# The first pair of FFN tiles closed before the second is opened, and the parameters turned between its two halves

## The chip, the cores and the metric

The kernel runs on one core of a Trainium2 chip. The metric is the device time of one execution in microseconds (us), taken as the median of several runs; lower is better.

## What is computed

The input x has 2048 tokens of 448 features (bf16). Two branches read the same x and are mixed token by token with a gate g; the result is bf16, 2048 x 448.

```python
g = sigmoid((x * gate_w).sum(-1, keepdims=True))
# branch a: a diagonal complex state-space model (S5), 448 states
dt = exp(log_dt);  Lam_bar = exp(dt * (Lambda_re + 1j * Lambda_im))
B_bar = ((Lam_bar - 1.0) / Lam)[:, None] * (B_re + 1j * B_im)
Bu = einsum("bld,pd->blp", x, B_bar)
h[t] = Lam_bar * h[t - 1] + Bu[:, t]          # for t in range(2048)
a = 2.0 * einsum("blp,dp->bld", h, C_re + 1j * C_im).real + x * Dskip
# branch b: a feed-forward network, 448 -> 1792 -> 448
b = einsum("bsf,fd->bsd", silu(einsum("bsd,df->bsf", x, w1)), w2)
return g * a + (1 - g) * b
```

## The kernel before

The tokens are cut into four chunks (tc = 0 to 3) of 512. x is held turned (`xT`, features on partitions), 448 features in four blocks of 128 rows of which the last two overlap, so that every contraction is made of half blocks of 64 rows.

**The x products** (`x_products`, matmuls on L733) give two kinds of output tiles of 128 x 512: `F` tiles (x times w1, then SiLU on ACT, L703, into `aT`) and `B` tiles (x times B, copied to `UG` by DVE or ACT, L710/L712). Tiles are taken in pairs. The two tiles of a pair lie in two banks of PSUM and run side by side, one on the upper 64 rows of TensorE's array and one on the lower 64. A pair needs 14 half blocks, done as 7 steps of two matmuls: a first half of 4 steps, `half(k, 0)`, and a second half of 3 steps, `half(k, 1)`. In the second half the two tiles have changed their places between upper and lower rows, so a matmul of the second half writes a bank which the other half of the array has just written. The second half therefore waits for the first half's last matmul (`.own = h == 1`: the one case in which `Waits.put` makes PE wait on its own semaphore). In the loop the first half of the next pair is put between the two halves of a pair. `wait` names the exception: for k - 1 in `wait`, pair k is closed before pair k + 1 is opened. `fill` names other work which is put behind half n of a given k.

The first call does F tiles 0 to 9 of chunk 0, the seven B tiles of chunk 0, F tiles 10 to 13, and the B tiles of chunk 1. Pair 0's first half alone is issued as two pieces of two steps, each with the waits for what it reads; every other half is one piece and waits at its beginning for all that it reads. w1 comes in five column cuts (`W1CUTS`), each in two transfers (the upper and the lower two row blocks), all on SyncE's (SP's) queue but one: cut 0 holds pair 0, cut 1 pair 1, cut 2 pairs 2 and 3, cut 3 pair 4 and one tile more.

**The parameters** (`parameters`, fill `PRMF`): log_dt, Lambda_re and Lambda_im land as three rows of `prm`, are turned by four small matmuls against the identity (L605, `prm_t`) so that states lie on partitions, and are copied to `pc` (L609). The fourth block of columns wants columns 384 to 447 twice, on partitions 0 to 63 and 64 to 127; a DVE copy (L607) writes the second set into `prm` ahead of the turning. From `pc` hang the step sizes (GpSimd, i.e. POOL, L612), the phases (DVE, L624 and L593 to L631), and the sine and cosine tables (ACT, L629 and L632).

**The scan** (`lanes(tc)`): DVE multiplies `UG` by COS and SIN (L774), runs seven scans (L806), POOL's queue casts their results back into `UG` by DMA, and DVE turns them into `H` (L774).

**The gates** (`gates(tc)`, priority `GPR[tc]`): DVE products x * gate_w (`xg`) and x * Dskip (L774); ACT sums (L906), tanh (L908), g and 1 - g (L909, L910), and g * x * Dskip (L913).

**The rest**: `ffn2(tb)` multiplies `aT` by w2 for 128 tokens (L844), ACT evicts it times 1 - g (`fe`, L850), POOL's queue adds it to `xnat` (L852). `readout_weights` scales C (ACT `ct`, L891/L892, not before the planned time `CTAT`; DVE L894). `readout(tb)` multiplies `H` by it (L865); the result goes out (L875 and SP's stores).

**What sets the order.** The kernel lists its operations, and a planner (`Plan.order`) orders them ahead of time, with costs and priorities written in the code. PE keeps the order in which the operations are listed; on ACT, DVE, POOL and SP the operation that can start first by the plan goes next, and among those that can start at once the one with the lower priority number (silu 2.5, sines 3, fe 7, gates and ct 8 on ACT; phases 0 to 3, gates `GPR`, lanes 20 + tc on DVE). At run time each engine does its list in that order, waiting on semaphores. The planner also gives out the eight PSUM banks.

Of the kernel before, what the change touches and what calls it, by code (L numbers as in the profile page):

```python
# [11 lines left out]
BF16 = DT.bfloat16  # L12
# [14 lines left out]
XT1K = 6  # L27
S0 = (0, 4, 1, 5, 2, 6, 3)
XT1 = "da"
XDMA = (1, 2, 3)  # L30
XAFT = ["PO1"]
LORD = "Bs w3 BQ BI w4 x1 g n1 w2 x2 C n2 n3".split()
BPE = ((3,4),)
TRATE = 2
MERGE = True
NHF = 10
# [3 lines left out]
GAT = 10  # L40
GEARLY = (2,)
GMID = ()
W1CUTS = [0,256,512,1024,1408,1792]
L2AT = 1
UDVE = (0, 1, 2, 3, 4, 5, 6)
OUTA = (8, 9, 10, 11)
PRMF = (1, 0)
PRMP = 9.7
CPP = 20.5
CTAT = 46.0  # L50
GPR = (14, 20.3, 20.4, 21.4)
CASTB = (360000, 360000, 360000)
XCOL = [0, 128, 256, 320]

# [254 lines left out]
def bass_gated_mix__ssm_conv_s5__dense_activation_silu__prompt_kernel(nc, A_x, A_Lambda_re, A_Lambda_im, A_B_re, A_B_im, A_C_re, A_C_im,  # L309
               A_log_dt, A_Dskip, B_x, B_w1, B_w2, gate_w, out):  # L310
    with ExitStack() as ctx:
# [3 lines left out]
        def sb(name, shape, dtype):  # L315
            return E(nc.sbuf_tensor(name, list(shape), dtype))
# [27 lines left out]
        ident = sb("ident", [128, 128], BF16)  # L344
# [5 lines left out]
        sgn = sb("sgn", [128, 1], F32)  # L350
        sturn = sb("sturn", [128, 1], F32)
        hpi = sb("hpi", [128, 1], F32)
        prm = sb("prm", [3, 512], BF16)
        eul = sb("eul", [128, 4], F32)
        pc = sb("pc", [128, 4, 4], F32)
        dtc = sb("dtc", [128, 4], F32)
# [31 lines left out]
        def bk(t, k=0):  # L388
            return ps[:, t.bank + k, :]
# [16 lines left out]
        def DVE(fn, r, w, cost, prio, tag=""):  # L406
            return P.add("dve", fn, r, w, cost, prio, tag=tag)
# [4 lines left out]
        def PE(fn, r, w, cost, tag=""):  # L412
            return P.add("pe", fn, r, w, cost, 0, tag=tag)
# [7 lines left out]

        w1cuts = W1CUTS

# [33 lines left out]
        def turn_x(tc, after=()):  # L457
            for c, n in ((0, 3), (3, 1)):
                turn(xT[:, tc, c:c + n, :], x2[tc * CH:(tc + 1) * CH, XCOL[c]:XCOL[c] + 128 * n], " ".join(f"xT{tc}_{q}" for q in range(c, c + n)), CH * 256 * n, 3.9 if n == 3 else 1.4, after)
# [138 lines left out]
        def parameters():  # L598

            prmn = [f"prm{k}" for k in range(3)]  # L600
            tkp = Ps()

            def prm_t(pe):
                for b in range(4):
                    r = pe.matmul(bk(tkp)[:, 4 * b:4 * b + 3], prm[0:3, 128 * b:128 * b + 128], ident[0:3, 0:3], start=True, stop=True)  # L605
                return r
            DVE(lambda e: e.tensor_copy(prm[:, 448:512], prm[:, 384:448]), prmn + ["xT0_211"], ["prm4"], 0.17, 0)  # L607
            PE(prm_t, prmn + ["prm4", "ident"], [tkp], 0.5, "prmT")
            DVE(lambda e: e.tensor_copy(  # L609
                pc[:, 0:3, :], bk(tkp)[:, 0:16].rearrange("p (b k) -> p k b", k=4)[:, 0:3, :]), [tkp], ["pc"], 0.2, 0)  # L610
            LDT, LRE, LIM = (pc[:, k, :] for k in range(3))
# [76 lines left out]
        def weights(tile, p0, p1, i):  # L688
            kind, tc, k = tile
            return w1s[p0:p1, i, k * 128:k * 128 + 128] if kind == "F" else BT[p0:p1, i, LCOL[k]:LCOL[k] + 128]  # L690
# [26 lines left out]
        def x_products(tiles, fill={}, wait=()):  # L717

            part = (list(zip([(i, 64) for i in (0, 1, 2, 3)], [(i, 0) for i in (0, 1, 3, 2)])),
                    list(zip([(i, 0) for i in (0, 1, 2)], [(i, 64) for i in (0, 1, 3)])))
            pairs = [tiles[t:t + 2] for t in range(0, len(tiles), 2)]
            toks = [Ps(2) for _ in pairs]

            def steps(k, h, a, z):
                def body(pe):
                    for n, cut in list(enumerate(part[h]))[a:z]:  # L730
                        for b, ((i, p0), tile) in enumerate(zip(cut, pairs[k])):
                            tc = tile[1]
                            r = pe.matmul(bk(toks[k], b), weights(tile, p0, p0 + 64, i), xT[p0:p0 + 64, tc, i, :],  # L733
                                          start=(h == 0 and n == 0), stop=(h == 1 and n == 2))
                    return r
                reads = [n for cut in part[h][a:z] for (i, _), tile in zip(cut, pairs[k])
                         for n in xn_of[tile[1]][i] + (w1n(tile[2], i) if tile[0] == "F" else btn[tile[2]])]
                return PE(body, list(dict.fromkeys(reads)), [toks[k]], (z - a) * PE_MM[512], f"{pairs[k][0][0]}{pairs[k][0][1]}")

            def half(k, h):  # L740
                if h == 0 and pairs[k][0] == ("F", 0, 0):
                    def zero(pe):
                        for n in range(NFILL):
                            for b, p in enumerate((slice(64, 128), slice(0, 64))):
                                r = pe.matmul(bk(toks[k], b)[:, 0:128], ones[p, 0:128], ones[p, 0:128], start=True, stop=True)
                        return r
                    PE(zero, [], [toks[k]], NFILL * 0.11, "fill")
                    steps(k, 0, 0, 2)
                    steps(k, 0, 2, 4)
                else:  # L750
                    steps(k, h, 0, len(part[h])).own = h == 1
                if h:
                    evict(pairs[k], toks[k])

            half(0, 0)
            for f in fill.get(-1, ()):
                f()
            for k in range(len(pairs)):
                order = [lambda: half(k, 1)] + [lambda: half(k + 1, 0)] * (k + 1 < len(pairs))
                for n, f in enumerate(order if k - 1 in wait else order[::-1]):  # L760
                    f()
                    for m in fill.get((k, n), ()):
                        m()
                for f in fill.get(k, ()):
                    f()
# [115 lines left out]
        def readout_weights(k):  # L881
# [15 lines left out]
        def gates(tc):  # L897
            xnn = ["xn00", "xn01"] if tc == 0 else [f"xn{tc}"]
            b4 = slice(4 * tc, 4 * tc + 4)
            tt(xg[:, :, :], xnat[:, b4, :], gwb[:, None, :].to_broadcast([128, 4, D_MOD]), ALU.mult,  # L900
               xnn + ["gwb"] + (["Gf0"] if tc else []), ["xg"], 1792, GPR[tc], "xg")
            tt(xnat[:, b4, :], xnat[:, b4, :], dkb[:, None, :].to_broadcast([128, 4, D_MOD]), ALU.mult,
               xnn + ["dkb"] + (["Gf0"] if tc else []), [f"xd{tc}"] + xnn, 1792, GPR[tc], "xd")
            for b in range(4):
# [11 lines left out]
        def xt(tc, who):  # L916
            return [lambda: x_transposes(tc, who)]
# [7 lines left out]
        def C(*tbs):  # L925
            return [lambda tb=tb: readout(tb) for tb in tbs]

        turn_b = [lambda a=a, z=z: b_transposes(a, z, "da") for a, z in BPE]
        NH = NHF
        K = NH // 2  # L930
        x_products(F(0, 0, NH) + B(0) + F(0, NH) + B(1),
                   {PRMF: [parameters], (K - 2, 0): turn_b[:1], K - 2: turn_b[1:2], K - 1: turn_b[2:], XT1K: xt(1, XT1) if 1 not in XDMA else [], 8: [lambda: lanes(0)] + [lambda: turn_x(3, XAFT)] * (3 in XDMA and bool(XAFT))}, [K - 2])
        gates(0)
        gates(1)
        for tc in GEARLY:
# [63 lines left out]
```

## Time and profile before

| | |
|---|---|
| median of 3 runs | 138.13 us (138.05 to 138.46) |
| the profiled execution | 138.0 us |
| its span, first to last instruction | 136.2 us |
| granted TensorE clock | 1.00 |
| PE, DVE, ACT, POOL busy | 97%, 87%, 65%, 31% of the span |
| matmuls of x products, L733 | 588 |
| matmuls of FFN 2, L844 | 224 |
| matmuls of the readout, L865 | 126 |

Reading it: times are from the span's start. PE is TensorE's matmuls, PEld its weight loads (which run beside matmuls), DVE VectorE, ACT ScalarE, POOL GpSimd, SP SyncE; a q behind an engine's name means its instruction queue, which issues DMAs and waits. A row of the timeline has the start, the length, engine, line, operation, names, shape and count of a group, and in brackets the engine's idle time ahead of it with what ended that. The chain of work that ended last is followed back from the end of the run, each piece to what released it. In a table by stage each engine has its busy time and its number of instructions, then the granted clock, the DMA engines' share and GB/s.

### The profile page before, as it was taken

Reading aid. Unit: us, or ns where it says so; the run is one execution under the profiler, and the core shown is the slowest. Engines: PE = TensorE matmul, PEld = TensorE weight load, DVE = VectorE, ACT = ScalarE, POOL = GpSimd, SP = SyncE. Lnnn points to the kernel's source line nnn. Section 1 sums busy time; section 2 is a strip of 40 time slices with the busy share of each in tenths; the row PEclk is TensorE's granted clock in tenths of the full one; section 3 lists DMA queues with packets and bytes.
Section 4 is the critical chain, followed back from the end, with each engine's and each line's share of the span. In section 5 each row is a group of like instructions: output and inputs, shape, how many; then the busy total and the mean of one; then the engine's idle time right before and its main releaser. Section 6 shows DMA issues by size and latency. Waiting matters only on the chain.

```text
span 136.2 us, 2554 instructions
## 1 busy us (share of the span) xinstructions
PE 132.4 (97%) x993; PEld 63.9 (47%) x993; DVE 118.5 (87%) x159; ACT 88.1 (65%) x155; POOL 42.0 (31%) x76
## 2 busy tenths in 40 slices
PE   7999999999999999999999999999999999999991
PEld 2444444444444555554444444445555555555561
DVE  0318999999997699999999999999999999999252
ACT  3238956999988997998476677699501117983200
POOL 7224030300346222224775020633100422346310
PEclk9999999999999999999999999999999999999999
DMA  4997989999999694222898010375712233229842
GB/s 125 334 240 135 205 129 262 343 176 155 206 212 234 110 183 75 36 34 34 119 141 155 3 39 0 54 110 109 153 65 95 39 52 49 32 38 130 171 108 68
DMA packets 29602, 16.87 MB, mean 124 GB/s; under 512 B 15123, under 2 KB 29462, under 8 KB 29590
## 3 DMA queue, kind: packets, MB, share of 16 engines
q1 hardware_dynamic: 22400, 10.38, 34.4%
q0 software_dynamic: 6640, 5.97, 29.2%
q10 hardware_dynamic: 550, 0.36, 0.8%
q8 instruction: 8, 0.13, 0.4%
q14 instruction: 4, 0.03, 0.1%
HBM read 5.62 MB, written 1.84 MB: 55 GB/s over the span
## 4 chain that ended last, share of the span: by engine, by line
PE 93%; DMA 3%; SPq 1%; issue 0%; DVE 0%
PE ps L733 46%; PE ps L844 31%; PE ps L865 16%; DMA w1s<-in_B_w_dram 3%; SPq L420 1%; DVE ot L875 0%; PE ps L605 0%; PE ps L673 0%
## 5 line engine op out<-in xcount | busy, mean ns | idle before, releaser
L733 PE MATMUL ps<-xT,w1s 64*128 64x512 bf16 x392 | 47.5, 376 | 0.3 <-DMA w1s<-in_B_w_dram 0.3
L844 PE MATMUL ps<-w2s,aT 128*128 128x448 bf16 x224 | 42.9, 352 | 0.0
L703 ACT ACTIVATE aT<-ps 128x1024 bf16<-128x1024 f32 (+1 forms) x30 | 28.7, 965 | 13.1 <-PE ps L733 12.9
L844 PEld LDWEIGHTS ps<-w2s,aT 128*128 128x128 bf16 x224 | 21.8, 98 | 20.7 <-issue 0.4
L733 PEld LDWEIGHTS ps<-xT,w1s 64*128 64x128 bf16 x392 | 20.0, 94 | 23.5 <-DMA w1s<-in_B_w_dram 0.7
L733 PE MATMUL ps<-xT,BT 64*128 64x512 bf16 x196 | 25.8, 376 | 0.0
L806 DVE TENSOR_TENSOR_SCAN Gf<-rc,gin,H 128x512 f32<-128x512 f32 x21 | 25.5, 1267 | 0.1
L852 POOL DMA_DIRECT2D xnat<-fe x16 | 13.8, 861 | 35.6 <-ACT fe L850 34.1
L420 POOL DMA_DIRECT2D UG<-Gf x27 | 15.0, 571 | 27.3 <-DVE Gf L806 26.8
L865 PE MATMUL ps<-CP,H 128*128 128x448 bf16 (+2 forms) x126 | 21.7, 332 | 0.0
L850 ACT ACTIVATE fe<-ps,g 128x448 bf16<-128x448 f32 x16 | 10.0, 626 | 17.8 <-PE ps L844 17.2
L865 PEld LDWEIGHTS ps<-CP,H 128*128 128x128 bf16 x126 | 11.6, 98 | 10.0 <-DVE Gf L806 0.4
L774 DVE TENSOR_TENSOR H<-UG,COS 128x3584 bf16<-128x3584 bf16 (+2 forms) x9 | 16.2, 1810 | 0.0
L733 PEld LDWEIGHTS ps<-xT,BT 64*128 64x128 bf16 x196 | 10.8, 94 | 11.5
L712 ACT ACTIVATE UG<-ps 128x1024 bf16<-128x1024 f32 (+1 forms) x12 | 10.7, 920 | 2.4 <-PE ps L733 2.4
L875 DVE SCALAR_TENSOR_TENSOR ot<-ps,g,xnat 128x448 bf16<-128x448 f32 (+2 forms) x14 | 8.1, 608 | 4.1 <-issue 2.8
L774 DVE TENSOR_TENSOR PO<-UG,SIN 128x1536 bf16<-128x1536 bf16 (+1 forms) x8 | 8.5, 1084 | 1.9 <-DMA UG<-Gf 1.9
L906 ACT ACTIVATE junk<-xg 128x448 bf16<-128x448 bf16 x16 | 9.2, 575 | 1.1 <-DVE xg L774 0.9
L420 POOL DMA_DIRECT2D UG<-UG x8 | 4.6, 575 | 17.1 <-ACT UG L712 9.6
L913 ACT ACTIVATE xnat<-xnat,g 128x448 bf16<-128x448 bf16 x16 | 9.7, 659 | 0.1
L774 DVE TENSOR_TENSOR PI<-UG,SIN 128x1536 bf16<-128x1536 bf16 (+1 forms) x8 | 8.6, 1086 | 0.0
L774 DVE TENSOR_TENSOR H<-H,PI 128x3584 bf16<-128x3584 bf16 x4 | 8.1, 2022 | 0.1
(93 smaller groups left out, 95.0 us busy)
## 6 DMA issues: line engine op xcount, KB each, us to landing
UG<-Gf POOLq DMA_DIRECT2D x21, 128.0 KB, 2.9
xnat<-fe POOLq DMA_DIRECT2D x16, 112.0 KB, 2.6
w2s<-in_B_w_dram SPq DMA_DIRECT2D x1, 1568.0 KB, 11.2
xnat<-in_A_x_dram SPq DMA_DIRECT2D x3, 448.0 KB, 5.9
out_dram<-ot SPq DMA_DIRECT2D x11, 112.0 KB, 1.7
w1s<-in_B_w_dram SPq DMA_DIRECT2D x4, 192.0 KB, 3.8
w1s<-in_B_w_dram SPq DMA_DIRECT2D x2, 256.0 KB, 4.3
UG<-UG POOLq DMA_DIRECT2D x8, 64.0 KB, 5.0
```

Of the source, the lines that this page charges most:

```text
L420: P.add(q, lambda e: e.dma_start(dst, src), list(after), name.split(), 0.6 if q == "pool" else 0.5 if nbytes > 2000 else 0.35, prio, sem() ...
L703: ACT(lambda e, src=src, dst=dst: e.activation(dst, src(), AF.Silu), [tk, "tbl"], [f"aT{tc % 2}_{m}" for m in names], act_cost(512 * n), 2 ...
L712: ACT(lambda e, src=src, dst=dst: e.activation(dst, src(), AF.Copy), [tk], after, act_cost(512 * n), 5, "U")
L733: r = pe.matmul(bk(toks[k], b), weights(tile, p0, p0 + 64, i), xT[p0:p0 + 64, tc, i, :], start=(h == 0 and n == 0), stop=(h == 1 and n == 2))
L774: DVE(lambda e: e.tensor_tensor(o, a, b, op), r, w, dve_cost(n, 2), prio, tag)
L806: DVE(lambda e, s=s, b=b, init=init: e.tensor_tensor_scan(Gf[:, s, :], rc[:, b:b + 1].to_broadcast([128, CH]), A[:, s, :], init, ALU.mult, ...
L844: r = pe.matmul(bk(tk)[:, 0:D_MOD], aT[tc % 2][:, fb, o:o + 128], w2s[:, fb, :], start=(fb == 0), stop=(fb == NFB - 1))
L850: ACT(lambda e: e.activation(f[:, :], bk(tk)[:, 0:D_MOD], AF.Copy, scale=g1[:, tb:tb + 1]), [tk, f"g1_{tc}"], [fn], act_cost(448, 1), 7, "fe")
L852: P.add("pool", lambda e: e.dma_start(Tb[:, tb, :], f[:, :], accum_op=ALU.add), [fn, f"Tb{tb}"], [f"Tb{tb}"], 0.94, 2, sem(), 250000, tag= ...
L865: r = pe.matmul(bk(tk)[:, 0:b - a], H[tc % 3][:, s, o:o + 128], CP[:, s, a:b], start=(s == 0), stop=(s == NSLOT - 1))
L906: ACT(lambda e, tb=tb, b=b: e.activation(junk[:, :], xg[:, b, :], AF.Copy, accum_out=zl[:, tb:tb + 1]), ["xg"], ["junk", f"zl{tc}"], act_c ...
L913: ACT(lambda e, tb=tb: e.activation(Tb[:, tb, :], xnat[:, tb, :], AF.Copy, scale=g[:, tb:tb + 1]), [f"xd{tc}", f"g_{tc}"], [f"Tb{tb}"], ac ...
```

## The change

Four things are done.

1. In the first call of `x_products` the exception list `wait` gets the member -1 (`EARLYW`), so that pair 0 is closed before pair 1 is opened. The order of halves on PE was (0,0) (1,0) (0,1) (2,0) turning (1,1) and becomes (0,0) turning (0,1) (1,0) (2,0) (1,1). From there on it is as before.
2. `PRMF` goes from (1, 0) to -1: the turning of the parameters stands directly behind pair 0's first half. `prm` has 448 columns; the fourth block is written by two matmuls of 64 columns each, one to partitions 0 to 63 and one to 64 to 127, and the DVE copy ahead of it is gone.
3. The first halves of pairs 1 and 2 (`k <= SPLIT`) are issued as two pieces of two steps.
4. The gates of chunk 0 get priority 20.3 in place of 14 (behind lanes(0) with 20, level with the gates of chunk 1), and ct may be planned from 43.0 in place of 46.0.

The diff, without lines in which only spaces differ:

```diff
-PRMF = (1, 0)
+PRMF = -1
+EARLYW = [-1]
+SPLIT = 2
 PRMP = 9.7
 CPP = 20.5
-CTAT = 46.0
-GPR = (14, 20.3, 20.4, 21.4)
+CTAT = 43.0
+GPR = (20.3, 20.3, 20.4, 21.4)
...
-        prm = sb("prm", [3, 512], BF16)
+        prm = sb("prm", [3, 448], BF16)
...
             def prm_t(pe):
-                for b in range(4):
-                    r = pe.matmul(bk(tkp)[:, 4 * b:4 * b + 3], prm[0:3, 128 * b:128 * b + 128], ident[0:3, 0:3], start=True, stop=True)
+
+                for b, p, c in ((0, 0, 0), (1, 0, 128), (2, 0, 256), (3, 0, 384), (3, 64, 384)):
+                    n = 128 if b < 3 else 64
+                    r = pe.matmul(bk(tkp)[p:p + n, 4 * b:4 * b + 3], prm[0:3, c:c + n], ident[0:3, 0:3], start=True, stop=True)
                 return r
-            DVE(lambda e: e.tensor_copy(prm[:, 448:512], prm[:, 384:448]), prmn + ["xT0_211"], ["prm4"], 0.17, 0)
-            PE(prm_t, prmn + ["prm4", "ident"], [tkp], 0.5, "prmT")
+            PE(prm_t, prmn + ["ident"], [tkp], 0.33, "prmT")
...
             toks = [Ps(2) for _ in pairs]
+            first = pairs[0][0] == ("F", 0, 0)
...
                     steps(k, 0, 0, 2)
                     steps(k, 0, 2, 4)
+                elif h == 0 and first and k <= SPLIT:
+                    steps(k, 0, 0, 2)
+                    steps(k, 0, 2, 4)
                 else:
...
-                   {PRMF: [parameters], (K - 2, 0): turn_b[:1], ...}, [K - 2])
+                   {PRMF: [parameters], (K - 2, 0): turn_b[:1], ...}, [K - 2] + EARLYW)
```

More of the change, by code (lines that the diff above doesn't have):

```diff
@@ L32 @@
 LORD = "Bs w3 BQ BI w4 x1 g n1 w2 x2 C n2 n3".split()
-BPE = ((3,4),)
+BPE = ((3, 4),)
 TRATE = 2
@@ L42 @@
 GMID = ()
-W1CUTS = [0,256,512,1024,1408,1792]
+W1CUTS = [0, 256, 512, 1024, 1408, 1792]
 L2AT = 1
@@ L931, in bass_gated_mix__ssm_conv_s5__dense_activation_silu__prompt_kernel @@
         x_products(F(0, 0, NH) + B(0) + F(0, NH) + B(1),
-                   {PRMF: [parameters], (K - 2, 0): turn_b[:1], K - 2: turn_b[1:2], K - 1: turn_b[2:], XT1K: xt(1, XT1) if 1 not in XDMA else [], 8: [lambda: lanes(0)] + [lambda: turn_x(3, XAFT)] * (3 in XDMA and bool(XAFT))}, [K - 2])
+                   {PRMF: [parameters], (K - 2, 0): turn_b[:1], K - 2: turn_b[1:2], K - 1: turn_b[2:], XT1K: xt(1, XT1) if 1 not in XDMA else [], 8: [lambda: lanes(0)] + [lambda: turn_x(3, XAFT)] * (3 in XDMA and bool(XAFT))}, [K - 2] + EARLYW)
         gates(0)
```

## The prediction

> **What bounds the kernel now.** I read the page first (busy shares), then the chain that ended last, then the start of that chain engine by engine, and last the rows where another engine comes near TensorE (PE).
>
> ```profile
> PE 132.4 (97%) x993; PEld 63.9 (47%) x993; DVE 118.5 (87%) x159; ACT 88.1 (65%) x155; POOL 42.0 (31%) x76
> ```
>
> PE is busy for 97% of the span. The chain in order of time says where that begins:
>
> ```profile
> 2.26 3.90 DMA w1s<-in_B_w_dram
> 6.16 0.14 issue
> 6.30 2.63 PE ps L733 x22
> 8.93 0.18 PE ps L605 x4
> 9.11 3.13 PE ps L733 x28
> ```
>
> From 6.30 us to 133.47 us the chain is PE alone. I went through the starts of all matmuls after 6 us: the intervals that are longer than the shape's own cadence (0.215 us for a step of L733) add up to 0.48 us in the whole run, 0.19 us of it before 9.04 us. So nothing after 9 us can be won; what this change can win lies in the first 9 us. There the chain hangs on one transfer: a w1 cut issued at 2.26 us lands at 6.16 us, and the second pair's first half starts 0.14 us later. The two rows of PE's timeline, weight loads and matmuls, show what PE did meanwhile:
>
> ```profile
> 5.42 0.11 PEld L733 LDWEIGHTS ps<-xT,w1s 64*128 64x128 bf16 x4 [0.34 <-DVE xT L553]
> 6.26 1.22 PEld L733 LDWEIGHTS ps<-xT,w1s 64*128 64x128 bf16 x14 [0.73 <-DMA w1s<-in_B_w_dram]
> 7.86 0.57 PEld L733 LDWEIGHTS ps<-xT,w1s 64*128 64x128 bf16 x8 [0.37 <-issue]
> 8.85 0.16 PEld L605 LDWEIGHTS ps<-ident,prm 3*128 3x128 bf16 x4 [0.42 <-issue]
> 9.04 2.70 PEld L733 LDWEIGHTS ps<-xT,w1s 64*128 64x128 bf16 x28
> ```
>
> ```profile
> 4.97 1.06 PE L733 MATMUL ps<-xT,w1s 64*128 64x512 bf16 x8
> 6.30 2.63 PE L733 MATMUL ps<-xT,w1s 64*128 64x512 bf16 x22 [0.26 <-DMA w1s<-in_B_w_dram]
> 8.86 0.25 PE L605 MATMUL ps<-ident,prm 3*128 3x3 bf16 x4
> 9.04 3.19 PE L733 MATMUL ps<-xT,w1s 64*128 64x512 bf16 x28
> ```
>
> The first row is pair 0's first half (4 steps of two matmuls side by side). It ends at 4.97 + 1.06 = 6.03; one matmul lasts 0.376, so its last step was issued at 5.65 and the next slot is 5.65 + 0.215 = 5.87. PE takes it only at 6.30: **0.43 us lost**. The x22 are 11 steps: pair 1's first half (4, from 6.30), pair 0's second half (3, from 7.16), pair 2's first half (4). The last four could have begun at 7.80, but began at 7.89: 0.09 us lost, because their weights came late. The two transfers that fill that cut, issued at 2.77 and 3.29:
>
> ```profile
> w1s<-in_B_w_dram SPq DMA_DIRECT2D x1, 256.0 KB, 4.2
> ...
> w1s<-in_B_w_dram SPq DMA_DIRECT2D x1, 256.0 KB, 4.5
> ```
>
> The upper half of the rows (2.77 + 4.2) is there at about 6.9, the lower (3.29 + 4.5) at 7.75. Then the parameters' turning: the slot after the 11 steps is 8.75, and the matmul after it starts at 9.04, so the four small matmuls take 0.29 of PE's time.
>
> **The change, part by part.** (1) *Order and turning.* Up to 5.87 nothing changes. Then come the turning, pair 0's second half (its weights have been in use since 4.97, so no transfer is waited for), pair 1's first half, pair 2's, pair 1's second half. The turning needs the parameters in SBUF. Their landing bounds it:
>
> ```profile
> 5.77 0.17 DVE L607 COPY prm<-prm 3x64 bf16<-3x64 bf16 x1 [0.40 <-DMA prm<-in_A_Lambda_im_dram]
> 9.14 0.17 DVE L609 COPY pc<-ps 128x12 f32<-128x12 f32 x1 [3.20 <-PE ps L605]
> ```
>
> The copy had waited for them and starts at 5.77, so they are there before 5.87. The turning now has five matmuls instead of four; one more small one is 0.025 (their starts are 0.025 apart), so 0.29 + 0.025 = 0.315 and pair 0's second half could go at 5.87 + 0.315 = 6.19. The two new 64-column forms are in no row. From below they cost nothing more. From above they cost one more change of shape: L733 to L605 loses 0.11, L605 back to L733 takes 0.09 where 0.025 is the small matmuls' spacing, so 0.07; L733 to L844 loses 0.10. I take 0.07 as the upper value (small matmul to something else is the nearest row): 6.19 to 6.26. [...]
>
> (2) *The wait that is added.* Pair 0's second half carries PE's wait on its own earlier half, and now no other pair stands between. The first half's end is 6.03; from a half's end to ACT's answer the trace has 7.97 to 8.09, 0.12, and a weight load precedes its matmul by 0.03, so it opens at about 6.18: just under the turning's end. The turning is its cover; without it 6.18 - 5.87 = 0.31 would be lost. Behind that wait on PE everything is queued, which is why it counts. [...]
>
> (3) *Sum.* Pair 0's second half starts at 6.19 to 6.26 and takes 3 steps, 0.645: 6.84 to 6.90. Pair 1's first half (landed 6.16) takes 4, 0.86: 7.70 to 7.76. Pair 2's first half is split: its first two steps need what landed at 6.9, its last two begin at 8.13 at the earliest and need what landed at 7.75 plus 0.14 = 7.89. So no wait: 8.56 to 8.62. Unsplit it would begin at 7.89, 0.13 to 0.19 later. Pair 1's second half then begins at 8.56 to 8.62 instead of 9.04: **a gain of 0.42 to 0.48 us, middle 0.45**.
>
> (4) *Downstream.* 0.45 stays if nothing is late. Later cuts of w1 land at 9.02 and 9.66 and are wanted at 10.7; the turned B at 10.8/11.8 and 14.4/14.9, wanted at 13.0 and 15.4; xT's second chunk at 19.0, wanted at 19.9. The DVE copy (0.17) goes, in a stretch where DVE idles 3.20: nothing. `pc` comes at about 6.45 instead of 9.14, and all that hangs on it (POOL's powers, DVE's phases, ACT's sines) may start 2.7 us sooner; DVE is full from 9 to 43 us, so it gains lead, no time. Its lead matters only at the end:
>
> ```profile
> 125.81 0.95 DVE L774 TENSOR_TENSOR H<-H,PO 128x1536 bf16<-128x1536 bf16 x1
> ...
> 127.97 0.54 PE L865 MATMUL ps<-CP,H 128*128 128x448 bf16 x2
> ```
>
> The last H is written at 126.76, 1.2 us ahead of its reader; with PE 0.45 earlier and DVE not moved at all 0.75 is left. (5) *GPR and CTAT.* The first chunk's gate products (two DVE passes of 1.08) may be passed by lanes(0), and ACT's gate work behind them (8 passes of L906/L913 and three small ones, 2.5 + 2.3 + 0.8 + 0.6 = 6.2 us between 26.1 and 42.3) slides later; ct's 8 passes may start 3 us sooner, wanted only by L865 at 90.9. I cost both at nothing; their cover is ACT's slack, and that is the second rival.
>
> The profiled run took 138.0 with a span of 136.2, near the median 138.13. 138.13 - 0.45 = 137.68; I say 137.67.
>
> **The rivals.** *A, the gain is eaten early (near 138.0).* ACT's sines now fall between 10 and 18 us, where it also empties the F pairs' banks. A SIN and COS pair is 0.63 + 0.72 = 1.35. The silu that frees pair 2's banks ended at 12.43 and the half that wants a bank began at 13.48: 1.05 of room. A silu behind such a pair costs 0.3: gain 0.15, time 137.98. For it: ACT would hold five silus of 1.02, eight sines and the rest in about 11 us. Against: the planner ranks silu (2.5) before sines (3), so at most one sine goes first.
>
> *B, slower: ACT becomes the bound at 63.6 us.*
>
> ```profile
> 26.10:42.28 16.18, 16.18 (x152) 7.11 (x146) 16.15 (x15) 15.09 (x27) 3.84 (x8) 1.00 1.14 207
> 42.28:63.60 21.32, 21.32 (x116) 10.90 (x116) 19.25 (x25) 20.02 (x47) 6.72 (x9) 1.00 0.59 94
> ```
>
> The fourth busy figure is ACT's: 20.02 of 21.32 in the stage in which PE does the first eight FFN-2 tiles. If half of the 6.2 slides into it, 20.0 + 3.1 - 21.3 = 1.8 spills over; if all, 4.9. The first F(2) pair starts at 63.58, and the weight load before it is put down to an fe eviction that ended 0.02 us before, so a late eviction there is paid in full: +1.8 - 0.45, time 139.5, up to 142.6. It decides once more than about 1.3 + 0.45 us of the sliding work stands ahead of the evictions. Against: evictions (rank 7) go before gates and ct (8), and ct's 5 us can wait past 63.6, where ACT is 67% busy.
>
> *C, more is won (near 137.35).* The timed runs reach 138.46; if w1 lands later in those than in the profile, the loss that goes is larger: up to 0.43 + 0.09 + 0.29 = 0.81.
>
> **How the numbers follow.** Forecast 0.58, A 0.14, B 0.21, C 0.07. A measurement of this kernel can tell about 0.3% from no change, 0.41 us, so faster means below 137.72. The forecast's own range (137.55 to 137.8) straddles that: 0.43 of its 0.58 lies below, as the upper value for the shape change leaves just 0.42. Faster 0.43 + 0.07 = 0.50; same 0.15 + 0.14 = 0.29; slower 0.21. The range goes from C's 137.3 to 138.6, which takes in A and a small B.
>
> **What would show it.** Right: no DMA wait of PE after 4.97; five L605 matmuls at about 5.98 ahead of a 3-step L733 row at 6.19 to 6.26; pair 1's second half near 8.6; `pc` near 6.45; every later PE row 0.4 to 0.5 sooner and the last matmul near 133.0. The 64-column cost is read from L605's last start to the next L733. Wrong: a PE wait on ACT near 13 or 63 us, on DVE at the last L865 block, or the turning starting late because the parameters land after 5.87.

## The result, and the profile after

The changed kernel takes 138.97 us (median of 6 runs, 138.92 to 139.53); the kernel before took 138.09 beside it (6 runs, 137.53 to 138.46). The ratio is 1.0076, with a 95% interval of 1.005 to 1.0102: slower by about 0.9 us, where 137.67 and a gain were forecast. Ratios, here and below, are made of undisturbed runs alone, so one of them can differ from that of the two medians beside it. The profiled run took 138.92 with a span of 137.0, against 138.0 and 136.2 before.

The lines of the changed kernel.py are some 3 to 7 higher, those of some runs below one or two more: the x products are L737 (L733), the turning L609 (L605), the DVE products L781 (L774), the scans L813 (L806), FFN 2 L851 (L844), `fe` L857 (L850), the readout L872 (L865), the evictions `ot` L882 (L875).

The first row of the page shows nothing of the loss: PE is busy for 97% of the span, DVE for 86% (87% before), ACT for 63% (65%).

**The part that was forecast came.** PE's timeline (start, length, line, shape, count):

```profile
4.94 1.06 PE L737 MATMUL ps<-xT,w1s 64*128 64x512 bf16 x8
5.93 0.34 PE L609 MATMUL ps<-ident,prm 3*128 3x3 bf16 x5
6.21 5.57 PE L737 MATMUL ps<-xT,w1s 64*128 64x512 bf16 x50
```

The turning follows pair 0's first half without a gap, and pair 0's second half starts at 6.21. From there 50 matmuls run with no wait for a DMA; pair 1's second half, the last of those that were reordered, begins at 8.60 where it began at 9.04. The first FFN-2 matmul starts at 41.83 against 42.28: 0.45 us gained, the forecast's number, and it is kept up to 66 us.

**Then it is lost, and more.** The waits (engine and line, what for: total, times, longest):

```profile
ACT junk L913 <- DVE xg L781: 6.8, 4, 3.8
...
DVE PO L781 <- DMA UG<-Gf: 3.8, 1, 3.8
...
DVE PI L781 <- DMA UG<-UG: 2.0, 1, 2.0
...
DVE ot L882 <- DMA xnat<-fe: 0.7, 1, 0.7
PEld ps L872 <- DVE H L781: 0.7, 1, 0.7
PEld ps L737 <- ACT fe L857: 0.6, 1, 0.6
```

The last two are PE's, and the kernel before had 0.4 for the one and nothing for the other. The source is DVE's. PI and PO are its products of `UG` with SIN, PI ahead of the scan and PO behind the casts of the scan's results. Its timeline after, the rows that matter between 20 and 50 us, the idle time ahead in brackets:

```profile
26.18 1.22 DVE L781 TENSOR_TENSOR PI<-UG,SIN 128x2048 bf16<-128x2048 bf16 x1 [2.00 <-DMA UG<-UG]
27.32 1.08 DVE L781 TENSOR_TENSOR xg<-xnat,gwb 128x1792 bf16<-128x1792 bf16 x1
...
31.25 7.91 DVE L813 TENSOR_TENSOR_SCAN Gf<-rc,H 128x512 f32<-128x512 f32 x7
...
44.51 0.96 DVE L781 TENSOR_TENSOR PO<-UG,SIN 128x1536 bf16<-128x1536 bf16 x1 [3.77 <-DMA UG<-Gf]
...
46.47 3.96 DVE L781 TENSOR_TENSOR H<-UG,COS 128x3584 bf16<-128x3584 bf16 x2
```

and before:

```profile
22.67 1.08 DVE L774 TENSOR_TENSOR xg<-xnat,gwb 128x1792 bf16<-128x1792 bf16 x1
...
28.10 2.09 DVE L774 TENSOR_TENSOR PI<-UG,SIN 128x1536 bf16<-128x1536 bf16 x2
30.10 2.02 DVE L774 TENSOR_TENSOR H<-UG,COS 128x3584 bf16<-128x3584 bf16 x1
...
34.09 7.92 DVE L806 TENSOR_TENSOR_SCAN Gf<-rc,H 128x512 f32<-128x512 f32 x7
...
45.49 0.96 DVE L774 TENSOR_TENSOR PO<-UG,SIN 128x1536 bf16<-128x1536 bf16 x1 [1.90 <-DMA UG<-Gf]
```

`UG<-UG` is the transfer that exchanges the two halves of the fourth block for lanes(0). It goes as two transfers, which land at 25.81 and 26.08 after and at 25.96 and 26.38 before; the lead that DVE has from the early parameters (`pc` at 6.32 instead of 9.14, 2.8 us) doesn't move it. Before, DVE did the gates' two passes (`xg` at 22.67, and `xnat` times Dskip at 23.85) in that time and waited for nothing. After, their priority puts them behind lanes(0): DVE stands still for 2.00 us and does them later, at 27.32 and 30.25. The casts `UG<-Gf` are the second wait. PO waits for the fifth of them: it is issued 2.84 us earlier (37.23 against 40.07) but lands only 0.98 earlier (44.39 against 45.37), and the last of the nine lands at 47.45 instead of 47.33. So most of DVE's lead turns into a wait of 3.77 instead of 1.90. The DMA share between 26 and 42 us is 1.23 after and 1.14 before in the table by stage; that the casts are slow for that reason is my guess, which no run sets apart.

PO itself starts earlier than before, and yet DVE is behind from there on, since another pass has moved: chunk 1's `H<-UG,COS`, 2.02 us, which stood at 30.10, now stands behind PO (the first of the two at 46.47). A lead of 0.98 less that pass is a lag of 1.04. The idle time says the same: idle time of DVE between 20 and 50 us is 5.77 against 1.90, 3.87 more; the lead of 2.8 covers all but 1.1 of it, and that is about what is seen at the end, where the last H is written at 128.09 instead of 126.76.

PE meets this in three places. (a) ACT waits for `xg` of a later chunk (3.8), and the `fe` evictions behind it in its list come late. There are two `fe` buffers: the eviction at 66.57 begins when the accumulation of the last but one has landed (66.46), and a pair of x products waits for its bank: 0.24 us of PE at 66.8. (b) The last readout tiles wait for H:

```profile
128.15 5.51 PE L872 MATMUL ps<-CP,H 128*128 128x448 bf16 x42 [0.23 <-DVE H L781]
```

That row began at 127.97 before; the lead of 0.45 has become a lag of 0.18, and the last matmul ends at 133.66 against 133.46. (c) The last piece of the chain of waits is new: the accumulation of the last `fe` into `xnat`, by POOL's queue, takes 4.82 us to land (3.08 before), and DVE's last evictions wait for it.

```profile
128.94 4.82 DMA xnat<-fe
```

The eviction of C15 (the last readout tile; C13 and C14 are the two ahead of it) begins at 133.78; it began at 132.79 before. Of the 0.99, PE's end makes 0.20, the transfer the rest. The table by stage shows what it ran beside (last two columns: DMA share, GB/s), before and after:

```profile
128.00:136.00 8.00, 5.46 (x43) 3.37 (x41) 2.99 (x6) 0.63 (x1) 0.85 (x1) 1.00 0.43 102
```

```profile
128.00:136.00 8.00, 5.51 (x42) 3.42 (x42) 3.08 (x7) 0.63 (x1) 0.84 (x1) 1.00 0.70 155
```

The readout's stores and the other accumulations were still under way: SP issued the four stores of `xnat` from 126.36 to 130.46 (before from 123.85 to 128.22), and the last accumulation of `ct` and the `fe` one behind it took 4.9 and 4.6 to land. The late H is not the only way to this: in e2 and e3 below the last H ends at 126.77 and 125.93, and the last accumulation still takes 4.02 and 4.08.

### The profile page after: what moved, and what is told of

Its sections match the earlier page's. It is cut to its first block, busy times and chain, and to the rows that moved or that the text cites. A ratio compares the mean times of both kernels' runs of the same rounds, so it can differ in the third digit from the quotient of the medians.

```text
span 137.0 us, 2551 instructions
## 1 busy us (share of the span) xinstructions
PE 132.3 (97%) x994; PEld 63.6 (46%) x994; DVE 118.4 (86%) x158; ACT 86.9 (63%) x155; POOL 42.1 (31%) x76
## 4 chain that ended last, share of the span: by engine, by line
PE 70%; DVE 10%; DMA 6%; POOL 4%; issue 4%; ACT 3%; DVEq 0%; POOLq 0%
PE ps L737 46%; PE ps L851 16%; PE ps L872 7%; DVE H L781 6%; DMA xnat<-fe 4%; POOL xnat L879 3%; DVE ot L882 2%; DMA xnat<-in_A_x_dram 2%; ACT UG L823 2%; POOL xnat L859 2%; ACT fe L857 1%; DVE Gf L813 1%; DVE PI L781 1%; PE ps L547 1%; DVE PO L781 0%
## 5 line engine op out<-in xcount | busy, mean ns | idle before, releaser
L737 PE MATMUL ps<-xT,w1s 64*128 64x512 bf16 x392 | 47.5, 376 | 0.1
L851 PE MATMUL ps<-w2s,aT 128*128 128x448 bf16 x224 | 42.9, 353 | 0.0
L851 PEld LDWEIGHTS ps<-w2s,aT 128*128 128x128 bf16 x224 | 21.8, 98 | 20.7 <-issue 0.4
L737 PEld LDWEIGHTS ps<-xT,w1s 64*128 64x128 bf16 x392 | 19.9, 94 | 23.3 <-ACT fe L857 0.6
L859 POOL DMA_DIRECT2D xnat<-fe x16 | 14.6, 914 | 40.7 <-ACT fe L857 38.5
L737 PE MATMUL ps<-xT,BT 64*128 64x512 bf16 x196 | 25.8, 376 | 0.0
L813 DVE TENSOR_TENSOR_SCAN Gf<-rc,gin,H 128x512 f32<-128x512 f32 x21 | 25.3, 1267 | 0.1
L872 PE MATMUL ps<-CP,H 128*128 128x448 bf16 (+2 forms) x126 | 21.7, 332 | 0.2 <-DVE H L781 0.2
L857 ACT ACTIVATE fe<-ps,g 128x448 bf16<-128x448 f32 x16 | 10.0, 625 | 13.3 <-PE ps L851 11.5
L872 PEld LDWEIGHTS ps<-CP,H 128*128 128x128 bf16 x126 | 11.6, 98 | 10.5 <-DVE H L781 0.7
L737 PEld LDWEIGHTS ps<-xT,BT 64*128 64x128 bf16 x196 | 10.8, 94 | 11.5
L781 DVE TENSOR_TENSOR H<-UG,COS 128x3584 bf16<-128x3584 bf16 (+2 forms) x9 | 16.1, 1813 | 0.0
L781 DVE TENSOR_TENSOR PO<-UG,SIN 128x1536 bf16<-128x1536 bf16 (+1 forms) x8 | 8.5, 1086 | 3.9 <-DMA UG<-Gf 3.8
L882 DVE SCALAR_TENSOR_TENSOR ot<-ps,g,xnat 128x448 bf16<-128x448 f32 (+2 forms) x14 | 8.2, 612 | 3.7 <-issue 1.6
L781 DVE TENSOR_TENSOR PI<-UG,SIN 128x1536 bf16<-128x1536 bf16 (+1 forms) x8 | 8.7, 1084 | 2.0 <-DMA UG<-UG 2.0
L823 ACT ACTIVATE UG<-Gf 128x512 bf16<-128x512 f32 (+1 forms) x9 | 5.6, 628 | 5.6 <-DVE Gf L813 5.5
```

The lines of the kernel that those rows point to most:

```text
L781: DVE(lambda e: e.tensor_tensor(o, a, b, op), r, w, dve_cost(n, 2), prio, tag)
L813: DVE(lambda e, s=s, b=b, init=init: e.tensor_tensor_scan(Gf[:, s, :], rc[:, b:b + 1].to_broadcast([128, CH]), A[:, s, :], init, ALU.mult, ...
L851: r = pe.matmul(bk(tk)[:, 0:D_MOD], aT[tc % 2][:, fb, o:o + 128], w2s[:, fb, :], start=(fb == 0), stop=(fb == NFB - 1))
L857: ACT(lambda e: e.activation(f[:, :], bk(tk)[:, 0:D_MOD], AF.Copy, scale=g1[:, tb:tb + 1]), [tk, f"g1_{tc}"], [fn], act_cost(448, 1), 7, "fe")
L859: P.add("pool", lambda e: e.dma_start(Tb[:, tb, :], f[:, :], accum_op=ALU.add), [fn, f"Tb{tb}"], [f"Tb{tb}"], 0.94, 2, sem(), 250000, tag= ...
L872: r = pe.matmul(bk(tk)[:, 0:b - a], H[tc % 3][:, s, o:o + 128], CP[:, s, a:b], start=(s == 0), stop=(s == NSLOT - 1))
```

## The experiments

**Which part costs: the order or the two numbers (e2, e3, e4).** e2 is the changed kernel with one number put back, e3 with both, e4 the kernel before with the two new numbers and nothing else.

```diff
 e2:
-GPR = (20.3, 20.3, 20.4, 21.4)
+GPR = (14, 20.3, 20.4, 21.4)
 e3, beside that:
-CTAT = 43.0
+CTAT = 46.0
 e4 (the kernel before):
-CTAT = 46.0
-GPR = (14, 20.3, 20.4, 21.4)
+CTAT = 43.0
+GPR = (20.3, 20.3, 20.4, 21.4)
```

> The changed kernel with the first gates' priority back at 14, ct still from 43. Rival 3 (gates of chunk 0 behind lanes(0) push chunk 1's COS product from the wait at 24 us to 48 us, so DVE ends 1.3 us later): the loss goes, 137.6. Theory 1 (any plan made with parameters 2.7 us sooner puts DVE and ACT out of step with the transfers): still slower than before, 138.4 to 139, with DVE waits of 3 us or more on transfers before 46 us.

> The changed kernel with both old numbers (first gates 14, ct from 46): only the order of the first pairs and the turning are new, and the planner plans anew. Theory 1: slower than before, 138.4 to 139. Rival 3 (the two numbers did it): 137.6.

> The kernel before with only the two numbers of the change (first gates 20.3, ct from 43): order of pairs, turning and copy as before. Rival 3: slower by 0.9 to 1.3, 139.0 to 139.4, since PE's 0.45 is missing too. Theory 1: near the kernel before, 138.0 to 138.4, as the parameters are no earlier and DVE reaches the transfers when they land.

| kernel | median | ratio to before, 95% |
|---|---|---|
| after (all of the change) | 138.97 | 1.0076 (1.005 to 1.0102) |
| e2: gates at 14 | 138.05 | 0.9996 (0.9977 to 1.0016) |
| e3: gates at 14, ct at 46 | 138.12 | 1.0002 (0.9986 to 1.0019) |
| e4: numbers only | 139.22 | 1.0086 (1.0055 to 1.0117) |

The two numbers alone cost what the whole change costs, and the gates' priority put back takes all of it away; `CTAT` makes no difference that these runs can tell. e2 and e3 lie between their two forecasts (137.6, or 138.4 and more): the loss goes, and no gain comes. e2's DVE shows the mechanism reversed: the gates lie ahead of the transfer's landing again, and PI starts without a wait.

```profile
21.05 1.09 DVE L781 TENSOR_TENSOR xg<-xnat,gwb 128x1792 bf16<-128x1792 bf16 x1 [0.52 <-DMA gwb<-in_gate_w_dram]
...
27.14 1.22 DVE L781 TENSOR_TENSOR PI<-UG,SIN 128x2048 bf16<-128x2048 bf16 x1
```

In e4 the wait for `UG<-UG` is there (2.25 us, at 27.21) and the last H ends at 128.57. But there the late gates reach PE by another way, and sooner:

```profile
ACT junk L906 <- DVE xg L774: 3.3, 2, 3.0
...
PEld ps L733 <- ACT aT L703: 2.1, 4, 1.0
```

`xg` comes at 30.44, ACT waits for it with the SiLU evictions behind the gates' sum in its list, and PE waits for their banks. FFN 2 starts at 43.23 instead of 42.28, and this 0.95 us stays to the end of PE's work (134.40 instead of 133.46). So the place of the gates is the cause in both kernels; that the two losses are of one size is partly chance, as they take different ways.

The order alone gains nothing (e3), although PE has a lead there (FFN 2 at 41.98). In its profile the end hangs on the last accumulation again: it lands at 132.91, and the eviction of C15 waits 0.37 us for it. Whether PE's start counts at all was the next question.

**Does PE's start set the end (e1, e8, e7)?** e1 has the new order on PE (the turning and pair 0's second half directly behind its first half) and no copy, and the other engines do the lists of the kernel before, less the copy; the first halves of pairs 1 and 2 stay split. e8 is e1 run once more for a profile. e7 is e1 with PE held up: four further matmuls of 256 columns behind the turning, whose results nobody reads.

```diff
 e1 (the kernel before, with the new prm_t and prm):
-        for o in P.order():
+        done = P.order()
+        pe = [o for o in done if o.eng == "pe"]
+        f0 = [o for o in pe if o.tag == "F0"]
+        turn = next(o for o in pe if o.tag == "prmT")
+        close = f0[4]
+        done = [o for o in done if o not in (turn, close)]
+        at = done.index(f0[1]) + 1
+        done[at:at] = [turn, close]
+        for o in done:
 e7, in prm_t:
+                for _ in range(4):
+                    r = pe.matmul(bk(tkp)[:, 256:512], ones[:, 0:128], ones[:, 0:256], start=True, stop=True)
```

> PE has the new order (turning, then pair 0's second half, then pair 1's first), five turning matmuls and no DVE copy, but DVE, ACT, POOL and SP keep the lists of the kernel before, entry for entry (less the copy). Theory 1 (the new lists of DVE and ACT lose the time: DVE comes to the half-swap and to the scan casts before these transfers have landed and has nothing else in its list there, and ACT's fe stands behind casts): PE keeps its 0.45 us to the end, so 137.6 against 138.1, DVE's last H no later than 126.8, no PE wait at the last readout block. Rival 2 (the earlier start itself does it, by transfers that collide, whatever the lists): slower than before, 138.5 or more. Rival 3 (the gate priority alone): 137.6 as well, since the gates are where they were.

> The kernel with the old lists once more, for a second profile: in the first one the clock opened only at 6.36 us and pair 0's first half ran at half speed, which took 0.6 us from PE's lead. With an early opening (before 5 us) PE reaches the FFN-2 tiles at 41.8 instead of 42.3. If its end is then still near that of the kernel before, the lead is lost behind PE; if the span is 135.7, it was the clock.

> The kernel of the run with the old lists, with four matmuls of 128x256 on constants behind the turning, which hold PE up by 0.43 to 0.5 us ahead of pair 0's second half and do nothing else. If PE's start sets the end in most runs, as the prediction had it: 138.45 to 138.5, 0.3% above the kernel with the old lists. If something else holds the end (transfers that set DVE's time, the last landing): 138.0 to 138.15, no change.

e1 took 138.02 (12 runs; ratio 1.0001, 0.9987 to 1.0015), e8 137.78, e7 138.62 (ratio 1.0033, 1.0018 to 1.0048). In e7's profile the x products go on 0.83 us after the turning's start (5.88 to 6.71), in e8's 0.28 (5.78 to 6.06). For these 0.55 us e7's ratio is 0.0032 above e1's, some 0.44 us: a delay of PE's start is paid to the end. So a gain there should show too, and e1's doesn't. The end of e1's chain says where part of it goes:

```profile
132.33 0.41 issue
132.74 0.17 DVE ot L882
```

DVE's wait for tile C14 is over at 132.33, but the eviction starts 0.41 us later, with nothing in the profile to wait for. e7 and e8 show the same 0.41 at the same tile; in the kernel before it is 0.04. These three profiles have 198 instructions on DVE (its queue's own counted), the kernel before 201; e2, with 200, has a delay of the same size one tile earlier, at C13 (131.22, where the cadence gives 130.86). In each of the three a packet of 8192 bytes on an instruction queue starts 0.65 to 0.7 us after that eviction; in the kernel before such a packet lies at 130.63, in a stretch where DVE waits for PE.

**Is it the copy's absence (e9, e10)?** e9 is e1 with the DVE copy kept, read by nobody. e10 is the kernel before, in its order, with the turning in five matmuls and no copy (and the first halves split, as in e1).

```diff
 e9 (e1 with):
-        prm = sb("prm", [3, 448], BF16)
+        prm = sb("prm", [3, 512], BF16)
...
+            DVE(lambda e: e.tensor_copy(prm[:, 448:512], prm[:, 384:448]), prmn + ["xT0_211"], ["prm4"], 0.17, 0)
             PE(prm_t, prmn + ["ident"], [tkp], 0.33, "prmT")
 e10 (the kernel before with the new prm_t):
-            DVE(lambda e: e.tensor_copy(prm[:, 448:512], prm[:, 384:448]), prmn + ["xT0_211"], ["prm4"], 0.17, 0)
```

> The kernel of e1 (pair 0 closed early, the turning in five matmuls that wait for no copy, the lists of the other engines those of the kernel before), but VectorE's 3x64 copy stays in its old place, read by nobody. TensorE's order is that of e1. Theory (the boundary): in e1, e7 and e8 VectorE lost 0.41 us ahead of the eviction of tile C14, near the end, where the kernel before loses 0.05, and an 8192-byte packet of the instruction queue follows it by 0.7 us; VectorE had 198 instructions there against 201. With the copy back the position returns to where VectorE waits for TensorE anyway: the eviction of C14 starts within 0.1 us of its wait's end, and the time is 137.6 to 137.7, ratio 0.996 to 0.997. Rival (the end doesn't hang on TensorE's start, or something else eats the gain): 138.0 to 138.1, ratio 0.999 to 1.000, with or without the 0.41.

> The other half alone: the kernel before in its order, with the turning in its old place, in five matmuls that read the 448 loaded columns, and without the 3x64 copy. TensorE's start is that of the kernel before, or 0.05 later for the fifth matmul. Theory (the boundary): the copy's absence alone moves VectorE's instructions forward, the eviction of C14 begins 0.4 us behind its wait's end, and the time is 138.4 to 138.6, ratio 1.002 to 1.0035. Rival (the copy's absence costs nothing): 138.05 to 138.15, ratio 0.9995 to 1.0005. A second rival (the copy held TensorE at 6.30): the turning starts up to 0.1 earlier, ratio 0.999.

e9: 137.73 (12 runs; ratio 0.9983, 0.9963 to 1.0004). e10: 138.30 (ratio 1.0021, 1.0007 to 1.0036). The eviction of C14 in e9, then in e10 (idle time ahead in brackets):

```profile
132.00 0.68 DVE L883 SCALAR_TENSOR_TENSOR ot<-ps,g,xnat 128x448 bf16<-128x448 f32 x1 [0.64 <-PE ps L873]
```

```profile
132.46 1.53 DVE L882 SCALAR_TENSOR_TENSOR ot<-ps,g,xnat 128x448 bf16<-128x448 f32 x4 [1.01 <-PE ps L872]
```

With the copy the idle time is 0.64, the usual cadence of PE's tiles; without it 1.01. A copy of 0.17 us at 5.8 us, whose result nobody reads, decides over 0.37 us at 132. e10's PE is not late (FFN 2 at 42.18, where the kernel before has 42.28), so neither the fifth matmul nor the split makes its loss. What the expectations call the boundary, a delay that goes with the count of DVE's instructions, holds in sign and place: it is there in e1, e7, e8 and e10 (198 instructions, C14 late by 0.41) and not in the kernel before (201, 0.04), where the packet at 130.63 lies in DVE's wait for PE from 130.23 to 130.88. That the packet is DVE's own, and that it makes the delay, was not shown, only that both move with the count. e9 reaches 137.40 to 137.57 in six of its twelve runs, but 137.90 to 138.57 in the other six; its interval reaches from the forecast (0.996 to 0.997) to no change, so a gain is not shown.

**What else eats it (e11 to e16).** e11, e12, e13 and e15 are e9's kernel again, each a single run with a profile. e14 and e16 are those of e5, the changed kernel, both numbers included, with one thing more: DVE's first `xg` and its `xnat` product are moved ahead of the PI that waits for `UG<-UG`.

```diff
 e5 (the changed kernel with):
-        for o in P.order():
+        done = P.order()
+        dve = [o for o in done if o.eng == "dve"]
+        xg0 = next(o for o in dve if o.tag == "xg")
+        xd0 = next(o for o in dve if o.tag == "xd")
+        late = next(o for o in dve if o.tag == "L0" and "PI_0" in o.writes)
+        done = [o for o in done if o not in (xg0, xd0)]
+        at = done.index(late)
+        done[at:at] = [xg0, xd0]
+        for o in done:
```

> The changed kernel with two entries of DVE's list moved: the first chunk's xg and xd stand ahead of the PI product that waits about 2.0 us (24.2 to 26.2) for the half-swap transfer, instead of behind it; every other list and all numbers stay. If the loss is that wait (the two passes, 2.1 us, had filled it in the kernel before): no DVE gap near 25 us, first scan 1.5 to 2 us sooner (29.3 to 29.8) or, if the casts' landing then holds DVE back instead, the last H at about 127 at best; time between 138.0 and 138.5. If the loss is in how ACT's list stands: no change, 138.9 to 139.2.

> The kernel of e9 again, for a profile. Its twelve times lay in two groups: 137.40 to 137.57 (five) and 137.90 to 138.57 (seven, among them the profiled one, 138.14). There the casts' transfers let PO start at 46.19, 0.7 later than in the kernel before, VectorE's last H ended 127.44 against 126.76, and the last accumulation took 4.13 us to land against 3.08, which held back the eviction of C15 by 0.57. Theory (the boundary, and the transfers of the lanes beside it): in a run of the lower group PO starts by 45.5, the last accumulation lands within 3.2 us, the evictions of C13 to C15 follow TensorE without a gap over 0.1, and the time is 137.4 to 137.6. In a run of the upper group the last accumulation takes 4 us or more. Rival: the groups differ in TensorE's start (the clock's opening), not at the end; then the first matmul of FFN-2 is 0.4 or more later in the upper group.

> As e11, the same kernel a third time: one more profile to set beside the other two.

> The kernel of e9 a fourth time. e11 (138.13) had no late transfers and the clock open only at 6.18, its turning at 6.51; e12 (138.65) had the clock open at 4.64 and the turning at 5.82, but PO started at 46.86 and the last accumulation took 4.62. Theory: the time is 137.4 to 137.6 where both go well (the turning by 5.9, PO by 45.5, the last accumulation within 3.2), and each of the two alone costs 0.5 to 1.0. Rival: a run with both well is still at 138.0 or more, and something further eats the 0.45.

> The kernel of e9 a fifth time, as e13: by the theory 137.4 to 137.6 where the clock opens early and PO starts by 45.5, and 0.5 to 1.0 more for each of the two that goes badly; by the rival 138.0 or more even where both go well.

> The kernel of e5 (all of the change, with two gate instructions of VectorE moved ahead of its wait for the half-swap) again, for a profile that is not the disturbed one. Theory: xg and xd lie at 20 to 24 ahead of the landing near 25.8; where PO starts by 45.5 the last H ends by 126.8 and the time is 137.3 to 137.6; where it starts at 46.5 or later it is 138.1 or more. Rival: the gap of 3.8 at PO, which the changed kernel showed, is there too and the last H ends at 128, with 138.5 or more in every run.

> The kernel of e5 once more, as e14: by the theory 137.3 to 137.6 where PO starts by 45.5, and 138.1 or more where it starts at 46.5 or later; by the rival 138.5 or more in every run, with a last H at 128.

e5 timed: 138.15 (10 runs, 137.32 to 139.76; ratio 0.9977, 0.9954 to 0.9999). Moving two instructions turns a loss of 0.8% into no loss, which confirms by a second way that the place of the gates ahead of that landing is what counts. In e16 they fill the wait:

```profile
23.95 1.08 DVE L781 TENSOR_TENSOR xg<-xnat,gwb 128x1792 bf16<-128x1792 bf16 x1
25.13 1.09 DVE L781 TENSOR_TENSOR xnat<-xnat,dkb 128x1792 bf16<-128x1792 bf16 x1
26.14 1.22 DVE L781 TENSOR_TENSOR PI<-UG,SIN 128x2048 bf16<-128x2048 bf16 x1
```

The profiles side by side, times in us (e3 and e2, then the four copy-kept runs and e9, then e8, then the two of e5's kernel):

| run | time | pair 0's first half took | turning starts | first FFN-2 | PO starts | last H ends | last accumulation took | C14 late by |
|---|---|---|---|---|---|---|---|---|
| before | 138.0 | 1.06 | 8.86 | 42.28 | 45.49 | 126.76 | 3.08 | 0.04 |
| e3 | 137.98 | 1.32 | 6.08 | 41.98 | 44.65 | 125.93 | 4.08 | 0.04 |
| e2 | 138.31 | 1.62 | 6.37 | 42.27 | 45.37 | 126.77 | 4.02 | 0.04, C13 by 0.41 |
| e15 | 137.91 | 1.45 | 6.28 | 42.18 | 45.40 | 126.67 | 3.44 | 0.04 |
| e11 | 138.13 | 1.63 | 6.51 | 42.40 | 45.83 | 127.08 | 3.20 | 0.04 |
| e9 | 138.14 | 1.26 | 6.19 | 42.09 | 46.19 | 127.44 | 4.13 | 0.04 |
| e13 | 138.22 | 1.05 | 5.92 | 41.80 | 46.47 | 127.73 | 4.38 | 0.04 |
| e12 | 138.65 | 1.07 | 5.82 | 42.10 | 46.86 | 128.13 | 4.62 | 0.04 |
| e8 | 137.78 | 1.06 | 5.78 | 41.68 | 45.37 | 126.63 | 3.04 | 0.41 |
| e16 | 137.47 | 1.04 | 5.79 | 41.68 | 43.31 | 127.00 | 3.85 | 0.04 |
| e14 | 138.73 | 1.07 | 5.77 | 41.65 | 44.63 | 128.09 | 4.53 | 0.04 |

Three things are told apart. *The clock's opening.* The same eight matmuls of pair 0's first half take 1.04 in e16 and 1.63 in e11:

```profile
4.82 1.04 PE L737 MATMUL ps<-xT,w1s 64*128 64x512 bf16 x8
```

```profile
4.94 1.63 PE L738 MATMUL ps<-xT,w1s 64*128 64x512 bf16 x8
```

In e11 a step takes 0.38 to 0.43 until 6.2 us (a start at 5.32, 5.75, 6.18) and 0.22 from then on; in e16 it is 0.21 to 0.22 from the first on. (The page's clock row shows full speed for both; the clock record kept with the trace begins at 6.18 in e11 and at 3.93 in e16.) Of 18 profiles of all kernels, 10 have 1.04 to 1.07 for this half and 8 have 1.16 to 1.74. The clock record begins at 3.38 to 4.64 in the ten and at 5.11 to 6.36 in seven of the eight; e9's trace has none. That is 2.6 to 5.6 us after the first matmul (at 0.76). The order of before doesn't pay for it: in e10, which has its order, that half took 1.53 too, and FFN-2 still began at 42.18; in the kernel before PE loses 0.43 at that place to the wait for w1. The new order has no wait left there, and in the runs with a late opening 0.5 to 0.7 of its lead is gone (first FFN-2 at 42.18 in e15 and 42.40 in e11, against 41.68 in e16).

*The casts.* Where they land late (PO at 46.2 to 46.9 in the copy-kept runs), the last H comes 0.7 to 1.4 later and the last accumulation takes 4.1 to 4.6 instead of 3.2 to 3.4; e13 has a good start (first FFN-2 at 41.80) and is at 138.22; e12's start is as good, but a stall of 0.37 at 15.1 lies ahead of its FFN-2. e14 and e16 run one kernel with the same start: the fifth cast lands at 44.51 and 43.19, the ninth at 48.09 and 47.15, and the last H ends 1.09 apart. By its forecast e14, with PO ahead of 45.5, should have taken 137.3 to 137.6; it took 138.73. The limit of 45.5 was wrong for this kernel: as in the changed kernel, chunk 1's `H<-UG,COS` still stands behind PO, so PO has to come some 2 us earlier than before to be level with it. In e16 it does (43.31), in e14 it doesn't, and there the wait at PO has grown to 5.72 and the last H ends at 128.09, as in the changed kernel. In that run filling the first wait has only lengthened the second. Why the casts land at different times in runs of one kernel is open, and so is the long last accumulation of e2 and e3, where H is not late.

*The boundary*: the 0.41 at C14, in e8 alone of these. No profile of the copy-kept kernel has an early clock and early casts at once, so that it then takes 137.4 to 137.6 is argued from its six faster runs, which have no profile. e16 comes nearest to a run with none of the three, and took 137.47, though its last accumulation took 3.85 too.

**One that missed (e6).** In the changed kernel ACT is idle for 4.98 us at 110.1, waiting for the last chunk's first scan, with an `fe` eviction behind the cast that waits. e6 puts that eviction ahead of it.

```diff
 e6 (the changed kernel with):
+        act = [o for o in done if o.eng == "act"]
+        cast = next(o for o in act if o.tag == "Gb")
+        fe = next(o for o in act[act.index(cast):] if o.tag == "fe")
+        done.remove(fe)
+        done.insert(done.index(cast), fe)
```

> The changed kernel with one entry of ACT's list moved: the fourth late fe eviction stands ahead of lanes(3)'s first cast (as in the kernel before) instead of behind it, where ACT idled 5.0 us (110.1 to 115.1). If the end is set by POOL's queue of accumulations (fe late, ct late, last landing 133.75): the last accumulation lands about 1 us sooner and the time is 138.3 to 138.5. If it is DVE's late H alone: no change, 138.9 to 139.2.

138.87 (ratio 1.0043, 1.0019 to 1.0068). The interval overlaps that of the changed kernel; its profile still has DVE's two waits (2.09 and 4.15) and the last H at 128.26. Its fall of the last accumulation to 4.29, from 4.82, is within what runs of one kernel show. So that place of `fe` does not make the late H, and whether it adds to the loss these runs can't tell.

## Why the prediction was wrong

By its own steps:

(1) *Order and turning*: right. No wait for w1; five small matmuls at 5.93; pair 0's second half at 6.21, in the forecast 6.19 to 6.26. The shape change cost 0.06 (the step to the first 64-column matmul is 0.089, where its neighbours have 0.025), close to the upper value of 0.07. Counted as in the prediction, from the slot at 5.84 to the next x product, the turning took 0.37, where 0.315 to 0.385 was forecast; that 6.21 is not nearer the upper end is due to a first half that began at 4.94, not 4.97. The step "up to 5.87 nothing changes" held in this run, but had one run's clock in it: a half of 1.06 is one of 1.04 to 1.74. That the gain came out at just 0.45 is in part luck.

(2) *The added wait* cost at most 0.03 (0.119 from the last small matmul to the next x product, 0.092 before), (3) *the sum* was right: 8.60 against 8.56 to 8.62, and 0.45 at the first FFN-2 tile.

(4) *Downstream* failed. "It gains lead, no time" took for granted that lead does no harm. The lead of 2.8 us ran into two sets of transfers that hardly moved with it (26.08 against 26.38, and 47.45 against 47.33), and the margin of 1.2 us between the last H and its reader, on which the whole step rested, was read from one run; over the copy-kept runs the last H lies between 126.67 and 128.13.

(5) *GPR and CTAT costed at nothing* is the step that decided, and failed. I named ACT's slack as the cover of the gates. It was DVE's: the gates were what DVE did while it waited for `UG<-UG`, and moved behind lanes(0) they leave 2.0 us of standing still, and a pass of 2.02 us goes behind the casts in their stead. The numbers alone cost 1.1 us (e4), about as much as the whole change, though there ACT's list passes the delay on to PE (0.95 us at FFN 2), which is the very cover that I had named. For CTAT the nothing was right (e2 against e3).

Rival A (early sines on ACT) did not occur. Rival B gave the sign, and partly the place, but not the mechanism: an `fe` eviction is late at 66.8 and costs 0.24, yet ACT is less busy than before in that stage (18.04 against 20.31 of the 22 us from 42 to 64); it waits for `xg`. Rival C (more is won than the profile shows) has its number near e16's 137.47, with the gates moved back; its ground, w1 landing later in the timed runs, was not looked at.

What I should have asked of step (5) is in the profile before: DVE shows no idle time ahead of the PI at 28.10, but the transfer that it needs has landed only at 26.38. Without the 2.2 us of `xg` and the `xnat` product DVE would have come there at about 25.9, and with the lead of 2.8 at about 23.1 (estimates from these rows).

## What to carry to other kernels

An engine that is full may be full because a planner put filler into a wait for a DMA. Before work of low rank is moved on such an engine, look up when the transfers behind its neighbours land: if these times don't move with the engine (here 26.08 against 26.38, for a lead of 2.8 us), the filler was free where it stood and may cost its full time elsewhere (here 2.00 us of standing still at PI, for 2.2 us of filler). And a gain at the start of a run reaches the end only where nothing later has a date of its own (here 0.45 us at FFN 2 was a lag of 0.18 at the last readout tiles); take the margins at the end from several profiles, since here the last H varied by 1.5 us in runs of one kernel.

## What the hardware showed that I had not expected

- A removed instruction of 0.17 us delayed another by 0.37 us 126 us later (e10 against before, e1 against e9): the eviction of C14 started 0.41 behind its released wait in four profiles with 198 instructions on DVE, and 0.04 behind it in those with 199 to 201.
- The clock record begins at 3.4 to 4.6 us in ten profiles and only at 5.1 to 6.4 us in seven, of the same kernel too (4.64 in e12, 6.18 in e11, where a step takes 0.38 to 0.43 until then and 0.22 after). In the order of before the first FFN-2 was not later for it (42.18 in e10, 42.28 in the kernel before); in the new order, without the wait for w1, it was later by 0.5 to 0.7 (e15 and e11 against e16).
- The last cast, issued 2.85 us earlier, landed 0.12 us later (47.45 against 47.33), in a kernel whose DMA share between 26 and 42 us was 1.23. The fifth landed 0.98 earlier.
- One transfer of 112 KB took 2.5 to 4.8 us to land at the end, longer where the stores lay in the same stretch (4.82 at 155 GB/s against 3.08 at 102). That the stores are the cause was not shown.
